# Moving query products, a modulation and weight loads one tile earlier in a decode kernel

## The chip, the cores and the metric

The kernel runs on one core of a Trainium2 chip. The metric is the device time of one execution in microseconds (us), as the median of several runs. A core has TensorE (PE in the profile), VectorE (DVE), ScalarE (ACT), GpSimd (POOL) and SyncE (SP), each with an instruction queue of its own that it works off in order, and 16 DMA engines that carry data between HBM and the on-chip memory.

## The reference, cut to what matters

One decode step of a block with four batch rows. An attention over a cache of 4096 keys, 32 heads of 128, comes first, then a small gated MLP; both are modulated by six vectors made from a condition `c`.

```python
mod = (_silu(c) @ w_mod).reshape(4, 6, 1, -1)
sa, ca, ga, sb, cb, gb = (mod[:, i] for i in range(6))
h = _layernorm(x) * (1 + ca) + sa
# attention: q = h @ wq; scores = q . k_cache * 128**-0.5; softmax; o = p @ v_cache; o @ wo
x = x + ga * _A_ref(h, A_k_cache, A_v_cache, A_wq, A_wo)
h = _layernorm(x) * (1 + cb) + sb
# gelu(h @ w_in), split in halves; layernorm of the second, times w_sp, plus b_sp; product @ w_out
x = x + gb * _B_ref(h, B_w_in, B_w_sp, B_b_sp, B_w_out)
```

K and V caches are 4 x 32 x 4096 x 128 in bf16, 134 MB each. All else is small: `wq` and `wo` 4.2 MB each, `w_mod` 3.1 MB.

## The kernel before, in words

**Tiles.** The work is cut into `NT` = 32 tiles. Tile `i` is one batch row `b = i % 4` and a group `g = i // 4` of four heads; its K and its V are 4 MB (4.19 million bytes) each, laid out as 128 partitions x 128 keys x 128. The loop `for i in range(NT)` issues, for tile i, the scores, and beside them the later steps of tiles i-1 (softmax), i-2 (product with V) and i-3 (masks and sums of the output).

**Scores.** TensorE has one query per head, so it can't make the scores well; VectorE multiplies K by the query spread over all partitions (`mult`, L303, in two halves), in place. The sum over the 128 elements of a head is done by TensorE with an identity matrix down to 8 partial sums (`reduce_d`, L311) that VectorE finishes (`sum8`, L330); for most of the second half VectorE sums alone (`sum_rest`, L323). `scores` takes maxima and exponentials (L339 to L352), `pv` multiplies with V on TensorE (L399).

**Queries.** `queries(n)` makes the spread queries `qbc` of one batch row and four head groups; there are eight such products, `n = half * 4 + b`. The first of a half (`n` = 0 and 4) also makes the rows of all four batch rows, 16 matmuls from `wq_sb` (L284) and a copy to `qrow`. Each product is one matmul (L290) and one ScalarE copy (L293). The PSUM tile `qps` has one buffer, so a product waits for the copy before it. Tile i needs product `(i // 16) * 4 + i % 4`: the first four tiles need 0 to 3, and 4 to 7 are first needed in tile 16. `QPLAN` says in which tile each is made: the first of a tile's list after `reduce_d(i, 0)`, the others after the second half's sums.

**Modulation.** `sa` and `ca` are made at the start. The block that begins with the two tiny loads into `sp_t` (L639, L640, on ScalarE's queue) makes `ga`, `sb`, `cb`: GpSimd clears `mrows` (which shares its single buffer, `osg`, with `qrow` and with the output masks of later tiles), 12 matmuls read `wm_sb` (L646), ScalarE copies three row blocks (L651), TensorE transposes (L654), VectorE copies to `modT` (L655). After it the pool `pre`, which holds `wq_sb` and `wm_sb`, is closed, and the projection weights `wo_sb` and `wo_last` get its place; their five loads (L666, L671) are issued there.

**Loads.** All large loads stand on one queue, SyncE's, and are issued in program order. K and V have two buffers each. `load_k(i + 2)` is issued in tile i behind `sum_rest(i)`, whose end frees the buffer, so SyncE waits there for VectorE. V of tiles 0 and 1 is issued before the loop and in tile 0; from tile 2 on tile i issues its own V behind `load_k(i + 2)`. Tile 1 issues no V. An issue also waits until the load that had its completion counter, eight issues earlier, has landed. The order is written out by hand; no scheduler changes it.

**The end.** After the loop come the last tile's output, the second layer norm and the MLP, with `win_sb`, `wout_sb` and the last modulation weights loaded behind the last V.

Of the kernel before, what the change touches and what calls it, by code (L numbers as in the profile page):

```python
# [27 lines left out]
def kernel(  # L28
# [271 lines left out]
    def mult(i, kc):  # L300
        kt = kts[i][:, kc * KC:(kc + 1) * KC, :]
        g, b = divmod(i, B)
        nc.vector.tensor_tensor(out=kt, in0=kt, in1=bc(qbc[:, g, b, :], KC), op=ALU.mult)  # L303

    def reduce_d(i, kc):
        ns = on_pe(i, kc)
        rd = 512 // ns
        kt = kts[i][:, kc * KC:kc * KC + ns, :]
        red = ps_red().rearrange("p (n r) -> p n r", r=rd)
        for m in range(DH // rd):  # L310
            nc.tensor.matmul(  # L311
                red, lhsT=ident_bf, rhs=kt[:, :, m * rd:(m + 1) * rd],
                start=(m == 0), stop=(m == DH // rd - 1),
            )
        st[i, "red", kc] = red
# [19 lines left out]
    def scores(i):  # L335
        sum8(i, 1)
        S = st.pop((i, "S"))
        mrow = wk.tile([P, 1], F32, name="mrow")
        nc.vector.tensor_reduce(out=mrow, in_=S, axis=AX.X, op=ALU.max)  # L339
        mb = wk.tile([P, R], F32, name="mb")  # L340
        nc.vector.tensor_scalar(  # L341
            out=mb, in0=mrow.to_broadcast([P, R]), scalar1=-att_scale, scalar2=None, op0=ALU.mult
        )
        mt = wk.tile([P, R], F32, name="mt")
        nc.vector.transpose(mt, mb)  # L345
        nM = wk.tile([P, 1], F32, name="nM")
        nc.vector.tensor_reduce(out=nM, in_=mt, axis=AX.X, op=ALU.min)  # L347
        pbd = pbds[i % 3]
        rs = wk.tile([P, 1], F32, name="rs", bufs=3)
        for q in range(HQ):  # L350
            r = slice(R * q, R * (q + 1))
            nc.scalar.activation(  # L352
                out=pbd[r, :, q], in_=S[r, :], func=AF.Exp, bias=nM[r, :],
                scale=att_scale, accum_out=rs[r, :],
            )
        st[i, "rs"] = rs
# [28 lines left out]
    def norm_b(i):  # L385
        if whole(i):
            z = st.pop((i, "z"))
            rz = wk.tile([P, z.shape[1], HQ], F32, name=f"rz{z.shape[1]}", bufs=2)
            nc.vector.reciprocal(out=rz, in_=z)
            st[i, "rz"] = rz  # L390
# [13 lines left out]
    def o_mask(i):  # L404
        osg = wk.tile([P, G, DH], F32, name="osg", bufs=1)
        for g in range(G):
            nc.scalar.activation(  # L407
                out=osg[:, g, :], in_=opss[i % 2][:, g, :], func=AF.Copy, scale=selg[:, g:g + 1]
            )
        st[i, "osg"] = osg  # L410

    def o_pick(i):
        ops = opss[i % 2]
        osb = wk.tile([P, DH], F32, name="osb", bufs=1)
        if i // B < NQ - 1:
            nc.vector.tensor_reduce(  # L416
                out=osb, in_=st.pop((i, "osg")).rearrange("p g d -> p d g"), axis=AX.X, op=ALU.add
            )
            st[i, "osb"] = osb
            return  # L420
        nc.vector.tensor_scalar(  # L421
            out=osb, in0=ops[:, 0, :], scalar1=selg[:, 0:1], scalar2=None, op0=ALU.mult
        )
        for g in range(1, G):
            nc.vector.scalar_tensor_tensor(
                out=osb, in0=ops[:, g, :], scalar=selg[:, g:g + 1], in1=osb,
                op0=ALU.mult, op1=ALU.add,
            )
        st[i, "osb"] = osb
# [141 lines left out]
    def rows_up():  # L571
        if "rows" in st:
            wp, k = st.pop("rows")
            if k == 0:
                nc.vector.tensor_copy(out=accR, in_=wp)
            else:
                nc.vector.tensor_tensor(out=accR, in0=accR, in1=wp, op=ALU.add)
            if SETS[k + 1] == HQ:
                st["turn"] = True
# [12 lines left out]
    def add_up():  # L592
        while adds:
            o_add(*adds.pop(0))

    QPLAN = {0: (1, 2), 1: (3, 4, 5), 2: (6, 7)}
    for i in range(NT):
        more = list(QPLAN.get(i, ()))
        mult(i, 0)
        if 3 <= i and (i - 3) // B < NQ - 1:  # L600
            o_mask(i - 3)
        if i >= 1:
            scores(i - 1)
        if i >= 2:
            norm_b(i - 2)
        add_up()
        rows_up()
        if i >= 3:
            o_pick(i - 3)
        dealt()  # L610
        reduce_d(i, 0)
        if i >= 3:
            o_cols(i - 3)
        if more:
            queries(more.pop(0))
        mult(i, 1)
        if i >= 1:
            norm_r(i - 1)
        if i >= 3:
            o_scale(i - 3)  # L620
        sum8(i, 0)
        reduce_d(i, 1)
        sum_rest(i)
        load_k(i + 2)
        if i >= 1:
            norm_a(i - 1)
        project()
        if i - 3 in ends:
            deal(ends[i - 3])
        while more:  # L630
            queries(more.pop(0))
        if i >= 2:
            pv(i - 2)
        if i == 0:
            load_v(1)
        elif 2 <= i < L:
            load_v(i)
        if i == 2:
            nc.scalar.dma_start(out=sp_t[:, 0:1], in_=B_w_sp[0:1, 0:1])  # L639
            nc.scalar.dma_start(out=sp_t[:, 1:2], in_=B_b_sp.rearrange("(a b) -> a b", b=1))  # L640
            mrows = wk.tile([P, G, DH], F32, name="osg", bufs=1).rearrange("p g d -> p (g d)")
            nc.gpsimd.memset(mrows, 0.0)
            mp = ps_sm([P, D])
            for k in range(DJ):
                for s in range(3):
                    nc.tensor.matmul(  # L646
                        mp[R * s:R * s + B], lhsT=cT[:, k, :], rhs=wm_sb[:, k, (2 + s) * D:(3 + s) * D],
                        start=(k == 0), stop=(k == DJ - 1), tile_position=(0, R * s),
                    )
            for s in range(3):  # L650
                nc.scalar.copy(out=mrows[R * s:R * s + B], in_=mp[R * s:R * s + B])  # L651
            mps = ps_sm([P, DJ, 3 * R])
            for j in range(DJ):
                nc.tensor.transpose(mps[:, j, :], mrows[0:3 * R, j:D:DJ], ident_f[0:3 * R, 0:3 * R])  # L654
            nc.vector.tensor_copy(  # L655
                out=modT.rearrange("p (s j) b -> p s j b", s=3),
                in_=mps.rearrange("p j (s r) -> p s j r", s=3)[:, :, :, 0:B],
            )
            pre_cm.__exit__(None, None, None)
            wts = tl = ctx.enter_context(tc.tile_pool(name="wts", bufs=1))  # L660
            wo_sb = wts.tile([P, H - HQ, D], BF16, name="wo_sb")
            wo_last = wts.tile([P, HQ, D], BF16, name="wo_last")
            hl = (H - HQ) * DH
            h0 = 0
            for n in SETS:
                nc.sync.dma_start(  # L666
                    out=wo_sb[:, h0:h0 + n, :],
                    in_=A_wo[h0 * DH:(h0 + n) * DH].rearrange("(p r) n -> p r n", p=P),
                )
                h0 += n  # L670
            nc.sync.dma_start(out=wo_last, in_=A_wo[hl:H * DH].rearrange("(q p) n -> p q n", p=P))  # L671
        if i == 5:
            sps = ps_sm([P, 2])
            nc.tensor.matmul(sps, lhsT=ones_b, rhs=sp_t, start=True, stop=True)
            nc.vector.tensor_copy(out=spf, in_=sps)
            nc.vector.tensor_copy(out=g8[:, 1, :], in_=spf[:, 0:1].to_broadcast([P, B]))
            cbT = modT[:, 2 * DJ:3 * DJ, :]
            nc.vector.tensor_scalar_add(out=cbT, in0=cbT, scalar1=1.0)
        if i == L - 1:
            load_v(L)  # L680
            win_sb = wts.tile([P, DJ, F], BF16, name="win_sb")
            win = B_w_in.rearrange("(p j) n -> p j n", p=P)
            for ks in KIN:
                nc.sync.dma_start(out=win_sb[:, ks], in_=win[:, ks])
            wout_sb = wts.tile([P, NH, D], BF16, name="wout_sb")
            nc.sync.dma_start(out=wout_sb, in_=B_w_out.rearrange("(j p) n -> p j n", p=P))
            wg_sb = kvp.tile([P, NJ, DH], BF16, name="vt", bufs=2)
            wg_sb = wg_sb.rearrange("p n d -> p (n d)")[:, 0:DJ * D].rearrange("p (k n) -> p k n", k=DJ)
            for ks in KG:
                nc.sync.dma_start(out=wg_sb[:, ks], in_=wm[:, ks, 5 * D:])  # L690
# [191 lines left out]
```

## Time and profile before

| What | Value |
|---|---|
| median of 3 runs (lowest to highest) | 668.01 us (667.84 to 668.31) |
| profiled execution: time, span | 667.8 us, 666.0 us |
| VectorE busy | 592.7 us (89% of the span) |
| TensorE matmul, weight load | 316.9 us (48%), 132.9 us (20%) |
| ScalarE, GpSimd busy | 128.2 us (19%), 4.4 us (1%) |
| DMA | 283.08 MB, mean 425 GB/s over the span |
| chain of waits | DMA 52%, VectorE 45%, TensorE 2% |

The span runs from the first to the last instruction of the profiled execution; its time also has what lies before and after. In the profile a row of the timeline gives start, duration, engine, line and operation, output and inputs, and in brackets the idle time of that engine before it with what ended it; adjacent instructions of a kind are merged to one row (x2). A row of a table by stretches gives its bounds and length, busy time and instruction count of PE, PEld (weight loads), DVE, ACT and POOL, the granted TensorE clock (1.00 is full), the share of the 16 DMA engines' time that was busy, and GB/s. A `q` behind an engine's name is its queue issuing a transfer.

### The profile page before, as it was taken

To read this page: it belongs to the slowest core of one execution; us is meant where nothing else is said; L and a number is where in the kernel's file an instruction comes from. 1 tells how busy PE (TensorE), PEld (TensorE's weight loads), DVE (VectorE), ACT (ScalarE), POOL (GpSimd) and SP (SyncE) were. 2 spreads that over 40 slices of the span, in tenths; PEclk is the share of its full clock that TensorE was granted. 3 is DMA by queue.
4 is the path that set the end of the run, shared out by engine and by line. 5 is a ranking of instruction groups with operands and counts; after the bars stand their busy time and mean duration, and the time that the engine had idled before them with its cause. 6 is when DMAs were issued, how large, how long until landed. Compare 5 with 4: busy or idle time off the path is not lost.

```text
span 666.0 us, 5470 instructions
## 1 busy us (share of the span) xinstructions
PE 316.9 (48%) x2132; PEld 132.9 (20%) x2132; DVE 592.7 (89%) x478; ACT 128.2 (19%) x423; POOL 4.4 (1%) x19
## 2 busy tenths in 40 slices
PE   1283455443445535334554344545433355564676
PEld 0131112111111212111121111211111122321335
DVE  3489899799999999999999999999999999999834
ACT  1021322121122212112221220222121122122112
POOL 1000000000000000000000000000000000000000
PEclk9996887667787667778866678887667888776976
DMA  8999999999999999999999999999999999999996
GB/s 364 452 429 425 378 425 435 431 436 437 428 429 437 436 430 429 434 437 434 425 435 438 431 425 436 439 431 425 437 434 435 425 436 437 431 428 428 441 414 266
DMA packets 13533, 283.08 MB, mean 425 GB/s; under 512 B 1340, under 2 KB 3268, under 8 KB 4420
## 3 DMA queue, kind: packets, MB, share of 16 engines
q1 hardware_dynamic: 13488, 282.73, 98.9%
q8 instruction: 16, 0.26, 0.1%
q14 instruction: 9, 0.07, 0.0%
q10 hardware_dynamic: 20, 0.01, 0.0%
HBM read 282.73 MB, written 0.00 MB: 425 GB/s over the span
## 4 chain that ended last, share of the span: by engine, by line
DMA 52%; DVE 45%; PE 2%; issue 1%; SPq 0%; ACT 0%; DVEq 0%
DMA kt<-in_A_k_cache_dram 46%; DVE kt L303 22%; DVE S L323 15%; DMA vt<-in_A_v_cache_dram 3%; DVE S L330 3%; DMA wout_sb<-in_B_w_out_dram 2%; DVE osb L416 2%; PE red L311 2%; DVE mrow L339 1%; DVE mt L345 1%; DVE mb L341 0%; DVE nM L347 0%; DVE oU L464 0%; PE ops L399 0%; DVE osg L527 0%
## 5 line engine op out<-in xcount | busy, mean ns | idle before, releaser
L311 PE MATMUL red<-kt,ident_bf 128*128 128x512 bf16 x676 | 221.4, 494 | 317.4 <-DVE kt L303 317.4
L303 DVE TENSOR_TENSOR kt<-kt,qbc 128x8192 bf16<-128x8192 bf16 x64 | 282.5, 4416 | 29.5 <-DMA kt<-in_A_k_cache_dram 29.1
L323 DVE TENSOR_REDUCE S<-kt 128x48 f32<-128x6144 bf16 x29 | 189.5, 6536 | 0.0
L311 PEld LDWEIGHTS <-ident_bf 128*128 128x128 bf16 x676 | 81.4, 120 | 454.2 <-issue 274.3
L352 ACT ACTIVATE pbd<-S,nM 32x128 bf16<-32x128 f32 x128 | 73.9, 577 | 302.7 <-DVE nM L347 290.1
L399 PE MATMUL ops<-vt,pbd 128*16 128x512 bf16 x992 | 64.3, 395 | 1.8 <-DMA vt<-in_A_v_cache_dram 1.8
L407 ACT ACTIVATE osg<-ops,selg 128x128 f32<-128x128 f32 x112 | 31.9, 368 | 165.7 <-PE ops L399 164.8
L330 DVE TENSOR_REDUCE S<-red 128x64 f32<-128x512 f32 x64 | 43.5, 680 | 6.7 <-PE red L311 6.7
L352 ACT ACTIVATION_READ_ACCUMULATOR pbd<-S,nM 32x1 f32 x128 | 32.2, 251 | 0.0
L399 PEld LDWEIGHTS <-pbd 128*16 128x16 bf16 x1008 | 24.0, 91 | 33.9 <-issue 12.7
L416 DVE TENSOR_REDUCE osb<-osg 128x128 f32<-128x512 f32 x28 | 28.1, 1005 | 0.0
L339 DVE TENSOR_REDUCE mrow<-S 128x1 f32<-128x128 f32 x32 | 9.2, 286 | 1.1
L293 ACT CAST qbc<-qps 128x512 bf16<-128x512 f32 x8 | 4.7, 585 | 22.3 <-PE qps L290 22.3
L364 ACT ACTIVATE rsb<-mask,rs 128x4 f32<-128x4 f32 x28 | 8.3, 297 | 1.0
L259 DVE SCALAR_TENSOR_TENSOR hs<-sm,xn 128x16 f32<-128x16 f32 x1 | 0.2, 174 | 9.1 <-PE sm L245 9.1
L345 DVE STREAM_TRANSPOSE mt<-mb 128x32 f32<-128x32 f32 x32 | 6.8, 211 | 1.1
L464 DVE TENSOR_REDUCE oU<-sm 128x4 f32<-128x128 f32 x28 | 7.7, 275 | 0.0
L434 PE MATMUL sm<-ident_f,osb 128*128 128x128 f32 x28 | 7.6, 273 | 0.0
L347 DVE TENSOR_REDUCE nM<-mt 128x1 f32<-128x32 f32 x32 | 6.0, 186 | 1.1
L341 DVE TENSOR_SCALAR mb<-mrow 128x32 f32<-128x32 f32 x32 | 5.8, 181 | 1.1
L421 DVE TENSOR_SCALAR osb<-ops,selg 128x128 f32<-128x128 f32 x4 | 1.4, 342 | 5.8 <-PE ops L399 5.8
L558 PE MATMUL sm<-wo_sb,od 128*4 128x512 bf16 x24 | 5.7, 379 | 0.0
(156 smaller groups left out, 104.5 us busy)
## 6 DMA issues: line engine op xcount, KB each, us to landing
kt<-in_A_k_cache_dram SPq DMA_DIRECT2D x31, 4096.0 KB, 19.9
vt<-in_A_v_cache_dram SPq DMA_DIRECT2D x31, 4096.0 KB, 29.3
wq_sb<-in_A_wq_dram SPq DMA_DIRECT2D x1, 4096.0 KB, 12.5
kt<-in_A_k_cache_dram SPq DMA_DIRECT2D x2, 2048.0 KB, 14.9
wo_sb<-in_A_wo_dram SPq DMA_DIRECT2D x3, 1024.0 KB, 26.1
kt<-in_A_v_cache_dram SPq DMA_DIRECT2D x3, 1024.0 KB, 26.6
wm_sb<-in_w_mod_dram SPq DMA_DIRECT2D x1, 2560.0 KB
win_sb<-in_B_w_in_dram SPq DMA_DIRECT2D x2, 896.0 KB, 23.8
```

The source lines that it names most:

```text
L303: nc.vector.tensor_tensor(out=kt, in0=kt, in1=bc(qbc[:, g, b, :], KC), op=ALU.mult)
L311: nc.tensor.matmul(red, lhsT=ident_bf, rhs=kt[:, :, m * rd:(m + 1) * rd], start=(m == 0), stop=(m == DH // rd - 1),)
L323: nc.vector.tensor_reduce(out=st[i, "S"][:, n0:NJ], in_=kts[i][:, n0:NJ, :], axis=AX.X, op=ALU.add)
L330: nc.vector.tensor_reduce(out=st[i, "S"][:, kc * KC:kc * KC + on_pe(i, kc)], in_=st.pop((i, "red", kc)), axis=AX.X, op=ALU.add,)
L339: nc.vector.tensor_reduce(out=mrow, in_=S, axis=AX.X, op=ALU.max)
L345: nc.vector.transpose(mt, mb)
L352: nc.scalar.activation(out=pbd[r, :, q], in_=S[r, :], func=AF.Exp, bias=nM[r, :], scale=att_scale, accum_out=rs[r, :],)
L364: nc.scalar.activation(out=st[g, "rsb"][:, b, :], in_=mask4, func=AF.Copy, scale=st.pop((i, "rs")))
L399: nc.tensor.matmul(opss[i % 2][g:g + G * HQ], lhsT=pbds[i % 3][:, n, :], rhs=vts[i][:, n, :], start=(m < 4), stop=(m >= end - 4), tile_pos ...
L407: nc.scalar.activation(out=osg[:, g, :], in_=opss[i % 2][:, g, :], func=AF.Copy, scale=selg[:, g:g + 1])
L416: nc.vector.tensor_reduce(out=osb, in_=st.pop((i, "osg")).rearrange("p g d -> p d g"), axis=AX.X, op=ALU.add)
L464: nc.vector.tensor_reduce(out=st[g, "o"][:, b, :], in_=op.rearrange("p (c q) -> p q c", q=HQ), axis=AX.X, op=ALU.add)
```

## The change

`QPLAN` makes all eight query products in tiles 0 and 1 (four more in tile 0, three in tile 1) and none in tile 2. The block with the two tiny loads, the modulation and the weight loads is entered at the end of tile 1 and not of tile 2. Since tile 2's end has `load_k(4)` and `load_v(2)` before that block, and tile 1's end has `load_k(3)`, the five weight loads now stand on SyncE's queue behind K of tile 3 and ahead of K of tile 4 and V of tile 2; before, they stood behind these two. VectorE's copy to `modT` stands ahead of tile 2's first product and not of tile 3's. Nothing is added or left out.

```diff
-    QPLAN = {0: (1, 2), 1: (3, 4, 5), 2: (6, 7)}
+    QPLAN = {0: (1, 2, 3, 4), 1: (5, 6, 7)}
     for i in range(NT):
         more = list(QPLAN.get(i, ()))
...
         elif 2 <= i < L:
             load_v(i)
-        if i == 2:
+        if i == 1:
             nc.scalar.dma_start(out=sp_t[:, 0:1], in_=B_w_sp[0:1, 0:1])
             nc.scalar.dma_start(out=sp_t[:, 1:2], in_=B_b_sp.rearrange("(a b) -> a b", b=1))
             mrows = wk.tile([P, G, DH], F32, name="osg", bufs=1).rearrange("p g d -> p (g d)")
```

## The prediction

> **What bounds the kernel now.** I read the stages first (busy time, DMA share and GB/s of each stretch):
>
> ```profile
> 2.00:76.00 74.00, 31.72 (x203) 13.54 (x203) 50.39 (x64) 14.42 (x35) 2.02 (x5) 0.93 1.00 428
> 76.00:82.00 6.00, 0.39 (x4) 0.33 (x3) 4.23 (x3) 1.14 (x4) 0.00 (x0) 0.57 0.75 268
> 82.00:642.00 560.00, 268.59 (x1661) 108.09 (x1660) 528.58 (x366) 108.00 (x374) 0.00 (x0) 0.75 1.00 432
> 642.00:662.00 20.00, 15.30 (x255) 10.47 (x256) 7.63 (x36) 4.27 (x10) 1.05 (x5) 0.62 0.93 373
> ```
>
> The last two columns carry the case. The DMA engines are full (share 1.00, 428 to 432 GB/s) from 2 to 642 us, but for one place, 76 to 82 us: share 0.75, 268 GB/s. VectorE, at 89% the busiest engine, has 528.6 us of work in the 560 us of the third row: it waits for data, not the data for it. So the transfers set the time, and a hole in their stream is lost for good.
>
> Why the hole is there, the issues on SyncE show:
>
> ```profile
> 43.69 0.33 SPq L107 DMA_DIRECT2D kt<-in_A_k_cache_dram  x1
> 44.06 0.43 SPq L107 DMA_DIRECT2D vt<-in_A_v_cache_dram  x1
> 58.35 18.82 SPq L107 DMA_DIRECT2D kt<-in_A_k_cache_dram  x2
> 77.27 0.38 SPq L107 DMA_DIRECT2D vt<-in_A_v_cache_dram  x1
> 77.82 2.67 SPq L666 DMA_DIRECT2D wo_sb<-in_A_wo_dram  x4
> 80.53 0.48 SPq L671 DMA_DIRECT2D wo_last<-in_A_wo_dram  x1
> 97.28 0.34 SPq L107 DMA_DIRECT2D kt<-in_A_k_cache_dram  x1
> ```
>
> These are K of tile 2, V of tile 1, K of tiles 3 and 4 (one row, the second at 77.16 - 0.33 = 76.8), V of tile 2, the weights, K of tile 5. Tile 1's end issues no V (`load_v(1)` is in tile 0, the next in tile 2), so from 58.4 to 76.8 us the engines have only the rest of V1 and K3, some 18 us of work. They run dry as K4 is issued. VectorE's rows show K3 and K5 landing:
>
> ```profile
> 70.24 6.54 DVE L323 TENSOR_REDUCE S<-kt 128x48 f32<-128x6144 bf16 x1
> 76.70 0.20 DVE L655 COPY modT<-sm 128x48 f32<-128x48 f32 x1
> 78.66 4.42 DVE L303 TENSOR_TENSOR kt<-kt,qbc 128x8192 bf16<-128x8192 bf16 x1 [1.77 <-DMA kt<-in_A_k_cache_dram]
> 120.13 4.43 DVE L303 TENSOR_TENSOR kt<-kt,qbc 128x8192 bf16<-128x8192 bf16 x1 [4.45 <-DMA kt<-in_A_k_cache_dram]
> ```
>
> Tile 3 waits 1.77 us for K3, tile 5 waits 4.45 us for K5. The end hangs on DMA too: the second last matmul group waits for `wout_sb`, last but one in the stream.
>
> **The queries (QPLAN).** Products 3 and 4 move to the end of tile 0, 5 to 7 to tile 1; none is added. A product is a matmul (0.38), a ScalarE copy (0.58) and, for number 4, a row block (16 matmuls, 1.05) and its copy (0.58). In tile 0 TensorE finishes its second reduction at 43.66. Product 2 then ends on ScalarE at 44.49, product 3 at 45.5; the row block runs 44.95 to 46.0, its copy to 46.6, product 4's matmul to 47.05, its copy to 47.65. Two things queue behind. Tile 1's first reduction, begun at 45.34, begins at 47.05; at its 3.61 us it ends at 50.7, before VectorE asks for it (51.14, L330). At the slow rate of tile 2 (4.94 us, granted clock 0.50) it would be 0.9 us late, and the 1.08 us for which tile 2 waits for K2 covers that. Tile 0's exponentials, from 46.99, start 0.7 us later; their reader, the PV product, runs at 70.9. In tile 1 product 5 takes the slot of 3, and 6 and 7 end by 54.5, an us sooner than 4 and 5 did. Tile 2 loses two products that ran beside VectorE's work. All zero.
>
> **The modulation.** Its rows before:
>
> ```profile
> 71.07 0.52 POOL L642 MEMSET osg<- 128x512 f32 x1 [67.57 <-PE qps L290]
> 72.67 1.03 PE L646 MATMUL sm<-wm_sb,cT 128*4 128x512 bf16 x12
> 73.81 1.75 ACT L651 COPY osg<-sm 4x512 f32<-4x512 f32 x3 [2.17 <-PE sm L646]
> 75.70 0.69 PE L654 MATMUL sm<-ident_f,osg 96*128 96x96 f32 x4 [2.00 <-ACT osg L651]
> ```
>
> They follow the last product's matmul, now at 53.9: matmuls to 55.0 with POOL's clearing beside them, ScalarE's two tiny loads (0.23 + 0.26) and copies to 56.9, transposes to 57.7. TensorE waits for those copies with nothing due behind it until 63.8, ScalarE has nothing until 65.48. VectorE's copy (0.20) stands between tile 1's sum, which ends at 58.28, and tile 2's first product, which waits for K2 until 59.36. If the transposes were 1 us late, the copy would still be hidden; beyond that each us is taken from the 1.77 us at tile 3. At its old place it also lay in a wait, so removing it gives nothing.
>
> **The weight loads.** Five issues (3.67 MB; 2.67 + 0.48 us on SyncE) go from behind K4 and V2 to behind K3. They need the last reads of the old buffers, the matmuls that end at about 55.0, so they go out at 58.8 to 62.0; K4, behind them on SyncE, is due at 76.8. Issues share eight completion counters in turn, so some wait for an older landing: the third for V0 (ahead of K2 in the stream), the fourth for K2 (59.3, so the last issues may slip by a fraction of an us), `wo_last` and K4 for the tiny loads. Before, these were issued at 71.06 and their packets ran at 75.28 and 76.50, 5.4 us at most; from 54.5 that is 60. Only a delay above 15 us would hold K4.
>
> So at 58.4 us the engines hold V1, K3 and the weights. The weights take 8.5 us at 432 GB/s, or 10 by the landings: V2 at 77.27 + 23.1 (median of its one issue) = 100.4, K5 at 120.1, less K5's own 9.7. They fill the stream to 87 to 88, and K4 comes at 76.8: no hole.
>
> What it is worth, from below: idle share, 0.25 x 6 = 1.5 us. From above: missing bytes, (432 - 268) / 432 x 6 = 2.3 us. Between them, the trace's packet records: of 16 engines the missing ones add up to 1.4 us each between 76.5 and 79.5, and the first packets of K4 took 1.8 to 2.2 us where 32 KB takes 1.21 (median), some 0.6 more: 2.0 us. I take 2.0, since it counts both the pause and the slow start.
>
> The Trainium skill (DMA: Bandwidth & Descriptors, Latency and other measured facts) gives about 0.6 us from issue to first byte on this path. By it a pause that began at about 76.8 with an issue at 76.8 would cost 0.6 and not 2.0, and the sum would be 667.4. The first packet of K4 is at 77.85, 1.0 us after its issue, and most came later and slow, so this trace does not agree. A time of 667.4 would be among those of the partial rival below.
>
> What is late next: K4, now behind the weights, lands at 78.5 + (8.5 to 10) + 9.7 = 96.7 to 98.2, where VectorE is free at 97.15: up to 1.0 us late. Tile 4 takes 18.5 us, so it ends by 116.7. V2 lands by 107.9, its reader runs at 109. K5 lands at 116.1 to 117.8 instead of 120.1, so tile 5 still waits and everything behind it moves forward. From there on the order is the old one: each K is issued with some 10 us of V queued (K7 at 138.9 landed 20 us later, 9.7 of it its own), so nothing runs dry.
>
> **Sum.** Span 666.0 - 2.0 = 664.0. The profiled execution took 667.8, 1.8 more than its span, and lies 0.2 under the median 668.0; against the median, 666.0. About 0.2% (1.3 us) can be told from no change.
>
> **Rivals.**
>
> The hole is paid elsewhere (partial). A landing is the slowest engine's. The engine that ended K3 last finished at 78.3 and could start on K4 almost at once; its gain is the rest of the pause (under 0.8) and the slow first packet (0.6), no more than 1.2: 666.8 to 667.6. For: K3 landed 1.5 us after most engines were done with it. Against: packets of 32 KB take 1.21 us on all engines, so none stays slow, and K5's landing is later by more than the mean.
>
> The Trainium skill (same page and section) says that engines 7 and 15 are usually slower than the rest. By it this rival would be the likelier; the packet records show no slower class.
>
> The pause also aligned the engines (slower). Without it the spread among them, which K3 (1.5 us) and the weights add to, runs on to the last load. Price: K5 landed up to 3.9 us after 16.25 MB at 433 GB/s would have (78.7 + 37.5 = 116.2); if such a spread is added at the end, 666.0 + 3.9 = 669.9. It decides once the added spread at `wout_sb` is above 2.0 us. For: the last stretch runs at 0.93, so there is a spread. Against: share 1.00 for 560 us, and pairs of tiles at a steady 38.7 us (158.84 to 197.58 to 236.29 on the chain of waits).
>
> No change: the code does what it says, in each engine's order, so only a stream that dries up again, for instance before K4, could leave 668. It needs the weights issued after about 76 us, 20 later than worked out.
>
> **Chances.** Hole closed, 0.76 (664.9 to 666.6). Partial, 0.14, all of it within 0.2%. No change, 0.03. Slower, 0.07. Range 664.9 to 667.5: the low end is a gain of 3.1, the middle of what K5's landing gives (2.3 to 4.0), the high end takes in most of the partial case. Faster 0.76, same 0.17, slower 0.07.
>
> **What would show it.** Right: DMA share near 1.00 at 76 to 82 us; five weight issues right behind K3 at 59 to 62; tile 5 starting at 117 to 118.3; the copy L655 near 58.3; K4's wait at tile 4 under 1 us. Wrong: a new stretch under 0.9 between 60 and 130, K4 issued later than 80, tile 5 at or after 120, or tile 5 early and the end not.

## The result, and the profile after

The changed kernel takes 665.85 us (median of 7 runs, 665.52 to 666.22), the kernel before 667.84 us beside it (667.73 to 669.19). The ratio of the means is 0.9966, 95% interval 0.9955 to 0.9978, so the gain lies between 1.5 and 3.0 us. The forecast was 666.0, in a range of 664.9 to 667.5, with the chance on faster. The profiled execution has a span of 664.1 us, 1.9 less than before.

The stages first, cut as before (busy time of the engines, then granted clock, DMA share, GB/s):

```profile
2.00:76.00 74.00, 33.02 (x204) 13.97 (x204) 50.38 (x65) 15.46 (x39) 2.03 (x5) 0.91 1.00 427
76.00:82.00 6.00, 0.00 (x0) 0.10 (x1) 4.66 (x2) 0.00 (x0) 0.00 (x0) 0.50 0.94 396
82.00:642.00 560.00, 266.39 (x1663) 107.60 (x1663) 528.93 (x368) 108.09 (x374) 0.00 (x0) 0.76 1.00 432
642.00:662.00 20.00, 14.68 (x265) 10.58 (x264) 8.13 (x38) 4.27 (x10) 1.05 (x5) 0.59 0.83 331
```

In the second row the share goes from 0.75 to 0.94 and the rate from 268 to 396 GB/s; the third row is what it was, 432 GB/s. A table counts a packet where it starts, so a row this short is blurred at its edges. The packet records have no such blur: between 4 and 644 us at least 16 packets, as many as there are engines, are under way at every moment, where the kernel before lacked 1.35 us of engine time (the mean over 16) at 76.5 to 79.5. The last row's share falls from 0.93 to 0.83 only because the stream ends 2 us sooner in it: its last packet is at 660.0 us, before at 661.9.

Now SyncE's issues, in the order K2, V1, K3, weights, K4, V2, K5:

```profile
42.98 0.33 SPq L107 DMA_DIRECT2D kt<-in_A_k_cache_dram  x1
43.35 0.43 SPq L107 DMA_DIRECT2D vt<-in_A_v_cache_dram  x1
57.65 0.33 SPq L107 DMA_DIRECT2D kt<-in_A_k_cache_dram  x1
58.15 1.75 SPq L666 DMA_DIRECT2D wo_sb<-in_A_wo_dram  x4
59.94 0.43 SPq L671 DMA_DIRECT2D wo_last<-in_A_wo_dram  x1
77.08 0.34 SPq L107 DMA_DIRECT2D kt<-in_A_k_cache_dram  x1
77.52 0.37 SPq L107 DMA_DIRECT2D vt<-in_A_v_cache_dram  x1
96.97 0.33 SPq L107 DMA_DIRECT2D kt<-in_A_k_cache_dram  x1
```

The weights go out half a microsecond behind K3, 17 us ahead of K4, which itself is issued no sooner than before. VectorE's rows show where the time is gained:

```profile
57.49 0.20 DVE L655 COPY modT<-sm 128x48 f32<-128x48 f32 x1
59.09 4.43 DVE L303 TENSOR_TENSOR kt<-kt,qbc 128x8192 bf16<-128x8192 bf16 x1 [1.41 <-DMA kt<-in_A_k_cache_dram]
69.86 0.69 DVE L330 TENSOR_REDUCE S<-red 128x64 f32<-128x512 f32 x1 [0.39 <-PE red L311]
78.35 4.43 DVE L303 TENSOR_TENSOR kt<-kt,qbc 128x8192 bf16<-128x8192 bf16 x1 [1.34 <-DMA kt<-in_A_k_cache_dram]
98.27 4.43 DVE L303 TENSOR_TENSOR kt<-kt,qbc 128x8192 bf16<-128x8192 bf16 x1 [1.36 <-DMA kt<-in_A_k_cache_dram]
117.59 4.42 DVE L303 TENSOR_TENSOR kt<-kt,qbc 128x8192 bf16<-128x8192 bf16 x1 [0.76 <-DMA kt<-in_A_k_cache_dram]
```

These are the modulation's copy and the starts of tiles 2, 3, 4 and 5, with one wait for TensorE in tile 2. Tile 3 starts as before (78.35 against 78.66), tile 4 later (98.27 against 97.15, now waiting for K4), tile 5 sooner (117.59 against 120.13). So a tile was made later and the kernel faster: what counts is when the stream has delivered, not when VectorE starts. From K7 on the old pattern holds, with K and V issued 2 to 3 us sooner (K7 at 136.31 instead of 138.85), and the span ends 1.9 us sooner.

### The profile page after: what moved, and what is told of

Its sections match the earlier page's. It is cut to its first block, busy times and chain, and to the rows that moved or that the text cites. A ratio compares the mean times of both kernels' runs of the same rounds, so it can differ in the third digit from the quotient of the medians.

```text
span 664.1 us, 5467 instructions
## 1 busy us (share of the span) xinstructions
PE 314.1 (47%) x2132; PEld 132.3 (20%) x2132; DVE 592.9 (89%) x478; ACT 128.2 (19%) x423; POOL 4.4 (1%) x19
## 4 chain that ended last, share of the span: by engine, by line
DMA 52%; DVE 45%; PE 2%; issue 1%; SPq 0%; ACT 0%; DVEq 0%
DMA kt<-in_A_k_cache_dram 46%; DVE kt L303 22%; DVE S L323 15%; DMA vt<-in_A_v_cache_dram 3%; DVE S L330 3%; DMA wout_sb<-in_B_w_out_dram 2%; DVE osb L416 2%; PE red L311 1%; DVE mrow L339 1%; DVE mt L345 1%; DVE mb L341 0%; DVE nM L347 0%; DVE oU L464 0%; PE ops L399 0%; DVE osg L527 0%
## 5 line engine op out<-in xcount | busy, mean ns | idle before, releaser
L399 PE MATMUL ops<-vt,pbd 128*16 128x512 bf16 x992 | 62.4, 387 | 1.4 <-DMA vt<-in_A_v_cache_dram 1.4
```

Source lines behind the costliest of these rows:

```text
L399: nc.tensor.matmul(opss[i % 2][g:g + G * HQ], lhsT=pbds[i % 3][:, n, :], rhs=vts[i][:, n, :], start=(m < 4), stop=(m >= end - 4), tile_pos ...
```

## The experiments

Two theories at first. The hole theory: only what the DMA engines have queued when K4 is issued counts. The compute theory: the gain comes from query products and modulation that no longer stand in tile 2. Each ratio below is that of the means to the kernel before, run beside it (median 667.88).

**Compute early, loads where they were.** The changed kernel with one line more, so that the pool is closed and the weights are issued in tile 2 again:

```diff
+        if i == 2:
             pre_cm.__exit__(None, None, None)
             wts = tl = ctx.enter_context(tc.tile_pool(name="wts", bufs=1))
```

> Query products and modulation as in the changed kernel, the five weight loads back behind K4 and V2. The hole theory (only the place of the loads counts): the DMA engines run dry at 76 to 78 us as before, 667.8 us against 667.8 of the kernel before. The theory that the earlier compute brings the gain: 665.9. Share of the stretch 76 to 82 us: 0.75 by the first, above 0.9 by the second.

Measured: 667.89 us, ratio 1.0000 (0.9991 to 1.0009). The stretch of the hole, and below it SyncE's issues of V2 and the weights in their old order:

```profile
76.00:82.00 6.00, 0.00 (x0) 0.10 (x1) 4.17 (x2) 0.00 (x0) 0.00 (x0) 0.65 0.75 268
```

```profile
77.21 0.38 SPq L107 DMA_DIRECT2D vt<-in_A_v_cache_dram  x1
77.75 2.63 SPq L667 DMA_DIRECT2D wo_sb<-in_A_wo_dram  x4
```

Share and rate are those of the kernel before to the digit. Moving the compute alone is worth nothing and costs nothing, within the 0.6 us of the interval: it only makes room for the weights.

**Another load in the hole.** The kernel before, with queries, modulation and weights untouched; in tile 2 the PV product and V2's load go ahead of the long sum and K4:

```diff
         sum8(i, 0)
         reduce_d(i, 1)
+        if i == 2:
+            pv(0)
+            load_v(2)
         sum_rest(i)
...
-        if i >= 2:
+        if i >= 3:
             pv(i - 2)
         if i == 0:
             load_v(1)
-        elif 2 <= i < L:
+        elif 3 <= i < L:
             load_v(i)
```

> The kernel before with its queries, modulation and weight loads where they were; only in tile 2 the PV product of tile 0 and the load of V2 go ahead of K4's issue. The hole theory: V2 is issued at about 72 us, the engines have 9.7 us more to do and do not run dry: 665.9. The compute theory: 667.8, nothing of it was moved. K4 lands at about 98 as in the changed kernel.

Measured: 665.99 us, ratio 0.9973 (0.9963 to 0.9983). SyncE's issues of V2, K4 and the weights, and below them the stretch of the hole:

```profile
72.99 0.33 SPq L107 DMA_DIRECT2D vt<-in_A_v_cache_dram  x1
77.31 0.33 SPq L107 DMA_DIRECT2D kt<-in_A_k_cache_dram  x1
77.82 1.75 SPq L672 DMA_DIRECT2D wo_sb<-in_A_wo_dram  x4
```

```profile
76.00:82.00 6.00, 0.69 (x4) 0.65 (x5) 4.69 (x3) 1.22 (x5) 0.00 (x0) 0.78 1.01 437
```

The whole gain comes back with none of the change's edits. V2, issued 3.5 us before the engines would have run dry, does what the weights did. The compute theory is out.

**How much is needed.** Two kernels with only a part of the weights ahead of K4, first the 512 KB piece, then the first 1 MB piece; the rest goes behind V2. The diff of the second is shown; `wo_last` stands in its new block too:

```diff
-            for n in SETS:
+            for n in SETS[:1]:
                 nc.sync.dma_start(
...
+        if i == 2:
+            for n in SETS[1:]:
```

> The changed kernel, but only the 512 KB weight piece stands ahead of K4 (1.27 us of the engines by the packet records), the other four loads behind V2. The hole theory: engines dry at 76.5 + 1.3 = 77.8 instead of 76.5, first packets of K4 at 78.1: 0.4 us of the 1.4 us pause is left, and perhaps the 0.6 to 0.8 us of slow first packets: 666.2 to 667.0. If the whole size of the weights counted (3.67 MB), a seventh of the gain: 667.5.

> The changed kernel, but only the first 1 MB weight piece stands ahead of K4 (2.5 us of the engines), the other four loads behind V2. The hole theory: dry only at 79.0, after K4's first packets could start at 78.1, so no pause: 665.9, the same as with all 3.67 MB. If the size of the weights counted, two sevenths of the gain: 667.3. K4 lands at about 91, so tile 4 does not wait for it.

Measured: 666.69 us with 512 KB, ratio 0.9984 (0.9976 to 0.9993), and 666.42 us with 1 MB, ratio 0.9983 (0.9975 to 0.9992). The stretch of the hole, 512 KB and then 1 MB:

```profile
76.00:82.00 6.00, 0.00 (x0) 0.11 (x1) 4.99 (x2) 0.00 (x0) 0.00 (x0) 0.55 0.87 322
```

```profile
76.00:82.00 6.00, 0.00 (x0) 0.10 (x1) 4.56 (x2) 0.00 (x0) 0.00 (x0) 0.50 1.04 410
```

512 KB, by the medians, brings over half of the gain. That piece is an eighth of the weights: the five loads are 4.19 MB, and the 3.67 MB that I had reckoned with leave out `wo_last`. An eighth or a seventh of the gain would be 0.3 us at most, and the interval begins at 0.5, so the size of the weights does not set the gain. By the packet records 512 KB leaves 0.85 us of pause and 0.65 us of slow first packets. But this trace is one of the longer executions (span 665.2, the median of its eleven is 664.8): VectorE waited 0.74 us for TensorE in tile 2, so that K4 was issued at 77.65, later than I had reckoned, and the usual pause should be shorter. With 1 MB only 0.03 us of pause is left, and yet 0.47 us of slow packets remain at K4's start. That fits a span of 664.5, 0.4 above the changed kernel's; in the medians the intervals overlap, so the difference is not clear of noise. The expectation of no loss at all was a little too good.

**A longer hole, with and without cover.** In both kernels VectorE's long sum of tile 2 is done twice ahead of K4's issue:

```diff
         sum_rest(i)
+        if i == 2:
+            sum_rest(i)
         load_k(i + 2)
```

> The kernel before, with VectorE's long sum of tile 2 (6.5 us) done twice ahead of K4's issue, so that K4 is issued 6.5 us later, at 83.4. The hole theory: the pause grows by 6.5, the time to 667.8 + 6.5 = 674.3. If a wait in the stream were made up later, or only VectorE's chain counted (tile 3 late by 6.5 - 1.8 = 4.7, tile 5 waits 4.4): 668 to 669.

> The changed kernel with the same second sum: K4 issued at 83.6. The hole theory: the weights keep the engines busy until 87 to 88, so no pause, 665.9, though tile 3 starts 5 us late and tile 5 3 us late; VectorE makes that up later, as it has about 1 us to spare in every two tiles. If lateness of VectorE's tiles passed to the end: 668.5 to 672.

Measured: the kernel before goes to 674.66 us, ratio 1.0099 (1.0085 to 1.0113), the changed one to 665.95, ratio 0.9973 (0.9964 to 0.9982). The former first: the stretch of the hole, K4's issue, and tile 5's start:

```profile
76.00:82.00 6.00, 0.84 (x4) 0.65 (x5) 5.97 (x2) 1.14 (x4) 0.00 (x0) 0.50 0.04 16
```

```profile
83.88 0.33 SPq L107 DMA_DIRECT2D kt<-in_A_k_cache_dram  x1
```

```profile
126.71 4.42 DVE L303 TENSOR_TENSOR kt<-kt,qbc 128x8192 bf16<-128x8192 bf16 x1 [5.86 <-DMA kt<-in_A_k_cache_dram]
```

The changed kernel with the second sum: the same stretch, the issues of K4, V2 and K5, and tile 5's start:

```profile
76.00:82.00 6.00, 0.00 (x0) 0.10 (x1) 5.97 (x2) 0.00 (x0) 0.00 (x0) 0.53 0.93 392
```

```profile
84.23 0.34 SPq L107 DMA_DIRECT2D kt<-in_A_k_cache_dram  x1
84.67 0.37 SPq L107 DMA_DIRECT2D vt<-in_A_v_cache_dram  x1
102.68 0.33 SPq L107 DMA_DIRECT2D kt<-in_A_k_cache_dram  x1
```

```profile
121.01 4.41 DVE L303 TENSOR_TENSOR kt<-kt,qbc 128x8192 bf16<-128x8192 bf16 x1
```

The same 6.5 us of work on the busiest engine costs 6.8 us in one kernel and nothing in the other. In the first K4 comes 7.0 us later (83.88 against 76.84) and the engines stand still for that time (share 0.04); it is never made up. In the second tile 3 starts at 84.07 instead of 78.35, 5.7 us late, and tile 5 at 121.01 instead of 117.59; the weights keep the stream full and VectorE catches up. So the change also leaves a reserve: K4 was issued 7.2 us later than in the changed kernel (84.23 against 77.08) at no cost.

**What the full stream is sensitive to next.** This is the changed kernel with `w_out` loaded in runs of 7 KB instead of 1 KB; the gate's columns are taken in steps of 7 so that the features match:

```diff
-            n0 = (h * NH + f) * P
+            n0 = h * FH + f
...
-                    zs[h][:, f, :], lhsT=win_sb[:, k, n0:n0 + P], rhs=hT2[:, k, :],
+                    zs[h][:, f, :], lhsT=win_sb[:, k, n0:n0 + (P - 1) * NH + 1:NH], rhs=hT2[:, k, :],
...
-            nc.sync.dma_start(out=wout_sb, in_=B_w_out.rearrange("(j p) n -> p j n", p=P))
+            nc.sync.dma_start(out=wout_sb, in_=B_w_out.rearrange("(p j) n -> p j n", p=P))
```

> The changed kernel, with w_out loaded as 128 runs of 7 KB instead of 896 of 1 KB (the gate's columns are taken in steps of 7 to match). In the full stream only the engines' time counts: 896 x 46 ns / 16 = 2.58 us becomes 128 x 272 ns / 16 = 2.18 us (both packet times from this trace), so 0.4 us less: 665.5. If the tail is bound by the compute between the last V and the end, no change (it was only 0.2 to 0.4 us ahead of w_out): 665.9; slower by some tenths if the strided weight loads on TensorE cost more.

Measured: 667.09 us, ratio 0.9987 (0.9978 to 0.9996), so 1.2 us slower than the changed kernel. The gate's matmuls and the product with `w_out`, in the changed kernel and then here, with the gate's weight loads (shortest, median and longest in ns) last:

```profile
656.34 1.63 PE L780 MATMUL red<-hT,win_sb 128*128 128x4 bf16 x56 [0.29 <-DVE hT L759]
...
658.96 0.91 PE L805 MATMUL qps<-zz,wout_sb 128*128 128x8 bf16 x28 [0.17 <-DMA wout_sb<-in_B_w_out_dram]
```

```profile
656.13 3.10 PE L780 MATMUL red<-hT,win_sb 128*128 128x4 bf16 x56 [0.29 <-DVE hT L759]
...
659.95 0.89 PE L805 MATMUL qps<-zz,wout_sb 128*128 128x8 bf16 x28 [0.21 <-DVE zz L798]
...
L780 PEld LDWEIGHTS <-win_sb x56: 131/153/153, 655.8 to 659.0; 128*128 128x128 bf16 x56
```

The transfers did get 0.4 us shorter (the times of all packets of 1 KB and more, over 16: 658.64 to 658.25). But the 56 matmuls with strided weight loads take 3.10 us instead of 1.63, and the bracket of the last row changes from DMA to VectorE: in the tail the compute is only some 0.2 us ahead of the stream, so it takes over at once. No version here beats the changed kernel.

## Why the prediction was right, step by step

**The bound.** DMA share and rate told it, and three experiments bear it out: the time followed the hole when it was closed by another load, left open, and made longer. The matmul group that waits for `wout_sb` (L805) is the third last, not the second last.

**The size.** I had bounded the hole between 1.5 us (idle share) and 2.3 us (missing bytes) and took 2.0 by the packet records. The runs give 1.99 (667.84 - 665.85), the spans 1.9, the last packet 1.96. That it fits to a hundredth is luck, as the interval is 1.5 us wide; the size is right within it. Its two parts are there singly: the pause of 1.35 us is gone, and the times of all packets of 1 KB and more, over 16, fall by 0.77 us (659.41 to 658.64), 0.71 of it the slow first packets of K4. The engines' idle time at the end grows by 0.18 and takes a little back.

**The restart.** A pause costs more than its idle time, as I had put it. In the kernel with the late K4, where the engines had long been dry, the first packet starts at 84.83, 0.95 us after the issue, and the first packets take 1.3 to 2.3 us instead of 1.21, 0.6 us in all. In the kernel before, K4's first packet starts at 77.80 (not 77.85), 0.96 us after the start of its issue. The Trainium skill (DMA: Bandwidth & Descriptors, Latency and other measured facts) has about 0.6 us to the first byte; by it the gain would have been 0.6 and not 2.0. Counted from the end of the issue's row, which is 0.33 us long, both traces give 0.62 to 0.63, so its figure may well be this part. What I had called a disagreement is then a matter of where the count begins; the gain of 2.0 has the rest of the pause and the slow packets as well.

**Queries and modulation at zero.** Right within 0.6 us, shown by the first experiment; and the V2 kernel, with the compute left in place, reaches 665.99. Product 4's copy ended at 46.9 and tile 1's first reduction at 49.7, ahead of VectorE's 50.43; the modulation's copy lay at 57.49 in the wait for K2. What I had missed is tile 2: its 20 reduction matmuls took 7.04 us, at a granted clock of 0.50 until 68.8 us, and VectorE waited 0.39 us for them (the row at 69.86). I had covered tile 1 against a slow clock, not tile 2. My slow rate was also too fast: in the row of 4.94 us the clock was at 0.50 only until 66.5, 0.72 on the mean. The 0.39 us came out of the wait for K3, which fell from 1.77 to 1.34. The moved products are not needed for such a wait: with the queries left in place, the kernel with V2 ahead shows 0.39 us and the one with the late K4 0.58.

**The weight loads.** Expected at 58.8 to 62.0, they went out at 58.15 to 60.4; no counter held them. Their size was wrong: `wo_last` (0.52 MB) is missing from the 3.67 MB, so they are 4.19 MB, 9.7 us at 432 GB/s and not 8.5, and 10.2 by their packet times. The 10 by the landings was the right end.

**What is late next.** K4's wait was mis-sized: up to 1.0 us said, 1.36 measured, as VectorE was free at 96.9 and K4 landed at 98.3, at the upper end of what I had worked out. It cost nothing, because tile 5 still waited for K5 (0.76 us), at 117.59 where I had said 117 to 118.3.

**The rivals.** The partial case held that the slowest engine's gain, at most 1.2 us, sets the end; the runs show the mean engine's. For engines 7 and 15 the Trainium skill (DMA: Bandwidth & Descriptors, Latency and other measured facts) gives as its best guess a cause that is specific to loads issued from GpSimd. These are issued from SyncE, so it hardly spoke for this rival. The spread among the engines without a pause to align them hardly grew: the idle time they have at the end before the last packet is 1.61 us against 1.43. The price of the rival that adds up this spread, 3.9 us, was too high as well: with 16.78 MB instead of 16.25 K5 would have been due at 117.5, and it landed 2.6 us after that.

## What to carry to other kernels

Where transfers bound a kernel, look for the one stretch in which the DMA share is below 1.00 and ask what was queued when it began; a load that can be issued ahead of the late one fills it, if it is long enough for the pause, and its being there in time is what counts. Even the busiest engine's added work can be free while the queue outlasts the delay and that engine has time to spare later (6.5 us cost nothing here); with the queue empty it cost its whole length (6.8 us). Compute that must be moved to free a buffer for an early load is priced by the waits that it lands in.

## What the runs showed of the hardware that was not expected

The slow start after a pause did not grow with its length here: the packet records give 0.71 us in the kernel before (1.4 us of pause), 0.62 us with a pause of some 8 us, and 0.6 to 0.7 us at the first load of every run. With 1 MB ahead of K4 there was hardly a pause and still 0.47 us, so standing still is not needed for it. K4's issue came 2.0 us before its first packet there, and 2.1 us before it in the changed kernel with the second sum, which lost only 0.06 us; so what sets this price stays open.

A TensorE weight load whose columns are 7 bf16 apart took 153 ns instead of 104 (median of 56); with columns 4 apart, in `wo_last`, it takes 118. The Trainium skill (SBUF — State Buffer, Door 1: The DMA port swizzle) says that memory lines are 16 bytes and that at least two accesses to each line are needed for the full rate. By that, steps of 4 elements (8 bytes) give two accesses and steps of 7 (14 bytes) about one. The 153 ns agrees with it, the 118 ns only in part, as contiguous columns take 104. No run varies the step alone, so the cause is not shown.
